# Fused pooled attention and residual MLP on one core: the first batch's loads, scores and order of parts rearranged

## The chip, the core and the metric

The kernel runs on one core of a Trainium2 chip. The metric is the time of one execution in microseconds of device time. Before the change three executions took 329.8, 329.99 and 332.36 us; the median is 329.99 us. A core has five engines that take their instructions in the order written: TensorE (PE, with its weight loads as PEld), VectorE (DVE), ScalarE (ACT), GpSimd (POOL) and SyncE (SP), and 16 DMA engines that move data. DMAs are issued from the queues of SP, ACT ("hardware" queues) or POOL ("software" queue; here the only one that converts fp32 to bf16 on the way).

## What is computed

Eight batches; eight heads of width 64, 576 rows, so 512 columns once the heads are side by side.

```python
def _attn_ref(q, k, v):                    # each (8, 8, 576, 64), fp32
    k_p = k.reshape(B, H, Sp, 8, D).mean(axis=3)      # 72 pooled rows
    v_p = v.reshape(B, H, Sp, 8, D).mean(axis=3)
    scores = scale * np.matmul(q, k_p.transpose(0, 1, 3, 2))
    attn = softmax(scores)                            # over the 72
    return np.matmul(attn, v_p)
def _moe_ref(x, ...):                      # x (8, 576, 512)
    a1 = alpha1 * x + beta1
    tok = np.einsum('ts,bsd->btd', w_tok, a1)         # w_tok 576 x 576
    u = x + lam * tok
    a2 = alpha2 * u + beta2
    ch = np.maximum(a2 @ w_ch1, 0.0) @ w_ch2          # 512 -> 2048 -> 512
    return u + lam * ch
```

## The kernel before

The 8 x 576 rows are cut into 36 chunks of 128, four to a block, nine blocks. While TensorE runs the MLP of block n, the attention of batch n + 1 and its token mix are put between its matmuls: `attention(b)` and the loop over blocks (L1187 on) give each part a due time, and the parts are issued in that order. Nothing overlaps with the attention of batch 0, so it is an opening of its own: the `plan` (L1082 to L1111) names its parts as generators, and the string `order` (L1113 to L1119) is the order in which they are advanced. A name that occurs twice is advanced twice: its matmuls at the first, the copy out of PSUM at the second. Each engine keeps its share of that order.

A head's rows 0 to 511 are laid out four to a partition ("c"), the last 64 rows are kept apart as remainder ("rem"), two to a partition and all heads together. The parts of the opening, by name:

- Loads ahead of the order (L414 to L457): lam and alpha1 on ACT's queue into one partition of `vecs`; the remainder rows of q and k, as fp32, on SP's and ACT's; q and k of heads 0 to 3 (`load_q_bf`, `load_k16`), v, then k and q of heads 4 to 7, v of these, w_tok, all with conversion on POOL's. Behind the constants: w1 (`load_w1(0)`, the first half of w_ch1) and batch 1's q (L1070 to L1072). k of batch 1 is k0, k1 in the order.
- d, dr, K: pooling k on TensorE. k's four rows per partition are paired c, c+1 (d copies row 0 behind row 3 to complete the ring), so that K (`att_K`) needs four matmuls a head. It writes `kpT`, in which the half of a head's query columns that belongs to the other row parity is zero.
- F, Fr: transposes of q (`att_F`, `att_Frem`).
- Sha, Shb (`scores`): the scores of one head, half by half: a matmul over 128 rows and 256 columns, with the remainder's 64 in the second half, then one exponential on ACT for each.
- V: pooling v. A: attention times v, a reciprocal and a product on DVE, into `x_tm`.
- s (`spread_lamal`): lam * alpha1, multiplied on one partition (L478), spread to 128 partitions by an fp32 matmul with a row of ones.
- X, R: x times lam*alpha1 into `xs`, main rows and remainder. b0, b1: the row lam * beta1.
- W, r: w_tok transposed, its row sums. M (`mix_T`): the token mix, plus x, times alpha2. T: its transposes. H, G: the first layer of the MLP for 256 and the other 256 tokens.
- la, ll, lr, lv, l1 to l4, k0, k1: loads of the vectors, remainder, v and k of batch 1, w_ch1 and w_ch2. wa: matmuls on zeros before there is data (`keep_warm`).

A tile of PSUM for a part in `in_pair` comes from two banks of their own, for the others from a pool of six.

## Time and profile before

| | us |
|---|---|
| median of three executions | 329.99 |
| profiled execution, time | 331.57 |
| profiled execution, span (first to last instruction) | 330.1 |
| around the span | 1.47 |
| first transpose of q begins (heads 0 to 3) | 8.24 |
| second load of q lands | 14.92 |
| first token-mix matmul of batch 0 begins | 22.38 |
| its result is read by VectorE | 23.67 |
| first matmul of the MLP begins | 28.16 |

Times are from the start of the span, durations in us unless marked ns. A row of the chain of waits has a start, a length and what lay on the chain; a row of the table by stretches has the stretch, its length, the busy time (and instructions) of TensorE, weight loads, VectorE, ScalarE and GpSimd, the granted TensorE clock, the share of the DMA engines and the GB/s that landed. The share can be above 1 when transfers stand in line. A row of the groups has the line, engine, operation, tiles and forms, count, then busy us and mean ns of one, then the idle time before them and what ended it. Engine busy time of TensorE is modelled and says little of its speed.

### The profile page before, as it was taken

Reading aid. Unit: us, or ns where it says so; the run is one execution under the profiler, and the core shown is the slowest. Engines: PE = TensorE matmul, PEld = TensorE weight load, DVE = VectorE, ACT = ScalarE, POOL = GpSimd, SP = SyncE. Lnnn points to the kernel's source line nnn. Section 1 sums busy time; section 2 is a strip of 40 time slices with the busy share of each in tenths; the row PEclk is TensorE's granted clock in tenths of the full one; section 3 lists DMA queues with packets and bytes.
Section 4 is the critical chain, followed back from the end, with each engine's and each line's share of the span. In section 5 each row is a group of like instructions: output and inputs, shape, how many; then the busy total and the mean of one; then the engine's idle time right before and its main releaser. Section 6 shows DMA issues by size and latency. Waiting matters only on the chain.

```text
span 330.1 us, 6467 instructions
## 1 busy us (share of the span) xinstructions
PE 323.3 (98%) x2469; PEld 206.7 (63%) x2469; DVE 235.9 (71%) x497; ACT 175.6 (53%) x324; POOL 115.5 (35%) x140
## 2 busy tenths in 40 slices
PE   7999999999999999999999999999999999999995
PEld 2677754455544576656775677558755866586584
DVE  5686276997779979786968797787788793263263
ACT  1785999358422961388128802782268225803710
POOL 8667535996247010900280027102510560000000
PEclk9999999999999999999999999999999999999999
DMA  7999989957996893499449943996560025003013
GB/s 107 194 220 290 284 172 222 203 147 174 170 261 108 201 180 105 82 266 181 144 95 230 196 150 80 176 214 148 135 178 0 2 53 159 0 2 127 0 34 95
DMA packets 73514, 47.72 MB, mean 145 GB/s; under 512 B 41181, under 2 KB 63845, under 8 KB 73482
## 3 DMA queue, kind: packets, MB, share of 16 engines
q1 hardware_dynamic: 58876, 34.50, 44.8%
q0 software_dynamic: 14000, 12.40, 22.5%
q10 hardware_dynamic: 606, 0.40, 0.5%
q8 instruction: 19, 0.31, 0.4%
q14 instruction: 13, 0.11, 0.1%
HBM read 38.57 MB, written 9.44 MB: 145 GB/s over the span
## 4 chain that ended last, share of the span: by engine, by line
PE 81%; DVE 7%; DMA 5%; POOL 3%; issue 1%; ACT 1%; SPq 0%; POOLq 0%; DVEq 0%
PE ps_h L931 34%; PE ps_w L1048 23%; PE ps_tok L880 10%; PE ps_ch L952 7%; DMA kT<-k_bf 2%; DMA q_bf<-in_q_dram 2%; PE ps_av L792 2%; PE ps_s L748 2%; DVE w L983 1%; DVE u_sb L885 1%; DVE x_tm L801 1%; DVE H L1017 1%; POOL k_bf L388 1%; DVE u_sb L1066 1%; POOL k_raw L386 1%
## 5 line engine op out<-in xcount | busy, mean ns | idle before, releaser
L931 PE MATMUL ps_h<-u_fm,w 128*128 128x512 bf16 (+2 forms) x608 | 132.7, 368 | 0.5 <-DVE u_sb L962 0.2
L939 ACT ACTIVATE H<-ps_h,bias_cols 128x512 bf16<-128x512 f32 x144 | 98.2, 688 | 55.2 <-PE ps_h L931 53.8
L931 PEld LDWEIGHTS <-w 128*128 128x128 bf16 x608 | 66.1, 114 | 50.7 <-issue 2.2
L1048 PEld LDWEIGHTS <-H 128*128 128x128 bf16 x560 | 53.5, 98 | 10.8 <-DVE u_sb L1066 1.2
L890 ACT CAST u_bf<-u_sb 128x512 bf16<-128x512 f32 x32 | 19.8, 618 | 70.7 <-issue 41.7
L1048 PE MATMUL ps_w<-w,H 128*128 128x256 bf16 x448 | 53.6, 273 | 0.0
L815 POOL TENSOR_TENSOR xs<-x_tm,lamal_bc 128x512 bf16<-128x512 f32 x11 | 13.9, 1270 | 104.8 <-DVE x_tm L801 104.7
L1066 DVE TENSOR_TENSOR u_sb<-u_sb,ps_w 128x512 f32<-128x512 f32 x54 | 36.4, 685 | 17.5 <-PE ps_w L1048 17.0
L880 PE MATMUL ps_tok<-xs,wtT 128*128 128x512 bf16 (+3 forms) x200 | 44.5, 380 | 0.0
L885 DVE TENSOR_TENSOR u_sb<-x_tm,ps_tok 128x512 f32<-128x512 f32 (+1 forms) x40 | 27.3, 684 | 8.9 <-PE ps_tok L880 8.9
L801 DVE TENSOR_TENSOR x_tm<-ps_av,recs 128x320 f32<-128x320 f32 x64 | 31.5, 492 | 2.8
L777 ACT ACTIVATE ET<-ps_s 72x512 f16<-72x512 f32 x56 | 32.3, 592 | 0.0
L952 PE MATMUL ps_ch<-w,H 128*128 128x512 bf16 x128 | 30.4, 379 | 0.0
L880 PEld LDWEIGHTS <-wtT 128*128 128x128 bf16 (+3 forms) x200 | 17.5, 100 | 16.4 <-issue 1.1
L717 DVE TENSOR_TENSOR v_u<-v_u 72x1024 f32<-72x1024 f32 (+1 forms) x24 | 23.6, 985 | 0.2
L799 DVE RECIPROCAL recs<-ps_av 128x5 f32<-128x5 f32 x64 | 12.1, 189 | 16.0 <-PE ps_av L796 15.8
L1048 PE MATMUL ps_w<-w_t,h_s 128*128 128x256 bf16 x168 | 22.6, 273 | 0.0
L952 PEld LDWEIGHTS <-H 128*128 128x128 bf16 x128 | 11.9, 97 | 13.7 <-issue 0.4
L386 POOL TENSOR_TENSOR k_raw<-k_raw 128x512 f32<-128x512 f32 x14 | 18.7, 1334 | 3.2 <-DMA k_raw<-in_k_dram 3.1
L388 POOL TENSOR_TENSOR k_bf<-k_raw 128x512 bf16<-128x512 f32 x14 | 19.1, 1364 | 1.1
L1017 DVE TENSOR_TENSOR h_s<-H 128x1024 bf16<-128x1024 bf16 x21 | 14.6, 697 | 6.3 <-ACT H L939 5.8
L1048 PEld LDWEIGHTS <-h_s 128*128 128x128 bf16 x168 | 16.4, 98 | 4.1
(165 smaller groups left out, 358.8 us busy)
## 6 DMA issues: line engine op xcount, KB each, us to landing
out_dram<-u_sb SPq DMA_DIRECT2D x29, 256.0 KB, 4.2
k_raw<-in_k_dram SPq DMA_DIRECT2D x12, 512.0 KB, 4.3
v_u<-in_v_dram SPq DMA_DIRECT2D x12, 512.0 KB
q_bf<-in_q_dram POOLq DMA_DIRECT2D x16, 256.0 KB, 5.9
w<-in_moe_w_ch_dram POOLq DMA_DIRECT2D x6, 512.0 KB, 14.4
out_dram<-u_sb SPq DMA_DIRECT2D x11, 128.0 KB, 2.2
w<-in_moe_w_ch_dram POOLq DMA_DIRECT2D x1, 1024.0 KB, 13.6
k_raw<-in_k_dram POOLq DMA_DIRECT2D x2, 512.0 KB, 14.7
```

The source lines that it names most:

```text
L386: eng.tensor_tensor(out=raw[:, :, 0:2], in0=raw[:, :, 0:2], in1=raw[:, :, 2:4], op=ALU.add)
L388: eng.tensor_tensor(out=bf, in0=twice[0], in1=twice[1], op=ALU.add)
L717: nc.vector.tensor_tensor(out=out, in0=t[:, :, 0:width], in1=t[:, :, width:2 * width], op=ALU.add)
L777: nc.scalar.activation(out=o, in_=i, func=AF.Exp, bias=0.0, scale=0.125 if b < 3 else 0.125 * 0.125)
L801: nc.vector.tensor_tensor(out=x[:, 1 - odd:6 - odd, dd:dd + D], in0=av[:, :, 0:64], in1=rec.unsqueeze(2).to_broadcast((P, 5, D)), op=ALU.mult)
L880: nc.tensor.matmul(out=ps_tok[p0:p1], lhsT=wtT[0:kk, at, P * c:P * c + p1 - p0], rhs=xs_pool[i][0:kk, sc, :], start=(sc == 0), stop=(sc == 4))
L885: nc.vector.tensor_tensor(out=s["u"][p0:p1, :], in0=x[p0:p1, 1 + c if c < 4 else 5 - 5 * i, :], in1=ps_tok[p0:p1, 0:DM], op=ALU.add)
L931: nc.tensor.matmul(out=ps_h[:, t0:t1 + one], lhsT=w1_of(cc, j), rhs=rhs, start=(cc == 0), stop=(cc == 3))
L939: nc.scalar.activation(out=H4[n, j // 4][:, j % 4, :], in_=ps_h, func=AF.Relu, bias=bias_cols[:, j:j + 1], scale=1.0)
L952: nc.tensor.matmul(out=ps, lhsT=H_of(n, j)[:, 128 * m:128 * m + 128], rhs=w2[j // 4][:, j % 4, :], start=(j == 0), stop=(j == NJ - 1))
L1048: nc.tensor.matmul(out=ps, lhsT=stat(j), rhs=moving(j), stop=(j == 7), start=(first and (pp == 0 or alone) and j == 0), skip_group_check=True)
L1066: nc.vector.tensor_tensor(out=o, in0=o, in1=banks[key, "both"], op=ALU.add)
```

## The change

All of it is in batch 0's opening, up to the first MLP block; the batches behind are issued as before.

- q of heads 0 to 3 comes as fp32 on ACT's queue into a tile that the MLP uses later (`load_q32`), and is cast by ScalarE in two parts (c0, c1). k of heads 0 to 3 comes as fp32 on SP's queue (`load_k`), and VectorE adds its rows (ks: `sum_k`, so far used for later batches), so that K0 has one matmul a head. Heads 4 to 7 keep the loads with conversion and d1. The remainder's q is cast by ScalarE (dq), its k added by VectorE (dr).
- SP's queue carries the small vectors; lam and alpha1 come as 12 rows (three copies of four pieces of 128). VectorE multiplies them and splits the product into three bf16 parts (vm), and four bf16 matmuls spread it.
- `kpT` is gone: `scores(p)` takes two heads in the two row halves (64 partitions each), with one exponential of 72x512 for each half (P0 to P3); the remainder's columns are Q0, Q1.
- Copies change engine: three of four qT copies, V1 to VectorE, K1 and the remainder's qT to ScalarE; X of heads 4, 5 to GpSimd, the remainder of heads 0 to 3 and the multiplication by alpha2 of chunk 0 to VectorE. Two memsets go to GpSimd.
- On POOL's queue the constants come first, then v, k and q of heads 4 to 7, v, w_tok. Then batch 1's first q (q0), w1 (l0), its second q (q1), k0 and k1, by their places in the order, which is new throughout.

```diff
@@ loads
+    def load_q32():
+        bf = work.tile([P, 4, 4, D], BF, tag="q_bf", bufs=4, name="q_bf")
+        raw = work.tile([P, 4, 4, D], FP, tag="H4", bufs=4, name="q_raw")
+        nc.scalar.dma_start(out=raw.rearrange("p h c d -> p h (c d)"), in_=rows(q, 0, 0))
+        st1[0]["q"][0], st1[0]["q_raw"] = bf, raw
+    def cast_q(r, copy):
+        pair = slice(2 * r, 2 * r + 2)
+        copy(out=st1[0]["q"][0][:, pair], in_=st1[0]["q_raw"][:, pair])
...
-    load_vector(0, moe_lam)
-    nc.scalar.dma_start(out=vecs[0:1, 2], in_=moe_alpha1.unsqueeze(0))
-    load_rem(0)
-    load_q_bf(0, 0)
-    load_k16(0, 0)
-    load_vector(1, moe_beta1, nc.sync)
+    load_q32()
+    load_k(0, 0)
...
+    load_rem(0, parts=((0, 0), (1, 0)))
+    load_rem(0, nc.scalar, parts=((0, 1), (1, 1)))
+    thrice = vecs[0:12, 2, 0:256].rearrange("p (i n) -> p i n", i=2)
+    for i, src in enumerate((moe_lam, moe_alpha1)):
+        nc.sync.dma_start(out=thrice[:, i], in_=src.rearrange("(c n) -> c n", n=P).unsqueeze(
+            0).to_broadcast((3, 4, P)))
+    load_vector(0, moe_lam, nc.sync)
+    load_vector(1, moe_beta1, nc.sync)
...
+    nc.gpsimd.memset(xs_pool[1][0:64, 4, :], 0.0)
+    nc.gpsimd.memset(vr16, 0.0)
...
@@ three parts
+    def which_part():
+        one = identity_bf[0:12, 0:12]
+        four = const.tile([12, 4], FP, tag="four", name="four")
+        nc.vector.tensor_reduce(out=four, in_=one.rearrange("p (k c) -> p c k", c=4), op=ALU.add,
+                                axis=AX.X)
+        nc.vector.tensor_copy(out=pick, in_=four.unsqueeze(2).to_broadcast((12, 4, P)))
+        for i in range(2):
+            nc.vector.tensor_reduce(out=less[:, i:i + 1], in_=one[:, 4 + 4 * i:], op=ALU.add,
+                                    axis=AX.X)
+        nc.vector.tensor_scalar(out=less, in0=less, scalar1=-1.0, scalar2=None, op0=ALU.mult)
+    def scale_vector(eng):
+        x = thrice[:, 0]
+        eng.tensor_tensor(out=x, in0=thrice[:, 0], in1=thrice[:, 1], op=ALU.mult)
+        for i in range(2):
+            eng.tensor_copy(out=part, in_=x)
+            eng.scalar_tensor_tensor(out=x, in0=part, scalar=less[:, i:i + 1], in1=x,
+                                     op0=ALU.mult, op1=ALU.add)
+        eng.tensor_copy(out=part, in_=x)
...
-        nc.tensor.matmul(out=ps, lhsT=ones_row, rhs=vecs[0:1, 2, cols])
+        for c in range(2):
+            nc.tensor.matmul(out=ps[:, 128 * c:128 * c + 128], lhsT=pick[:, 2 * half + c],
+                             rhs=part)
@@ pooled k and scores
-        for a, copy in enumerate(copies):
-            yield
-            rows = slice(64 * a, 64 * a + 64)
-            copy(out=kpT_pool[u][rows, a], in_=kp[rows])
+        yield
+        copy(out=kp_pool[u], in_=kp)
...
+    def scores(p):
+        st, u, i = st1[0], p // 2, 2 * p % 4
+        ps = [gp("ps_sc") for _ in range(2)]
+        for h in (i, i + 1):
+            for a in range(2):
+                rows = slice(64 * a, 64 * a + 64)
+                nc.tensor.matmul(out=ps[a][0:SPG, 256 * (h - i):256 * (h - i) + 256],
+                                 lhsT=kp_pool[u][rows, h, :],
+                                 rhs=st["qT"][u][rows, 2 * h:2 * h + 2, :])
+        for a in range(2):
+            yield
+            nc.scalar.activation(
+                out=ET_pool[u][:, i:i + 2, 256 * a:256 * a + 256],
+                in_=ps[a][0:SPG, :].rearrange("p (h i) -> p h i", i=256),
+                func=AF.Exp, bias=0.0, scale=0.125)
...
@@ order
-    load_w1(0)
-    load_q_bf(1, 0)
-    load_q_bf(1, 1)
-    warmed = keep_warm(16)
-    cast_rem(0, nc.vector)
+    warmed = keep_warm(14)
+    which_part()
...
-    for i, copy in enumerate((scalar, scalar, scalar, vector)):
+    for i, copy in enumerate((vector, vector, vector, scalar)):
...
-    for c, eng in enumerate((nc.gpsimd, nc.vector, nc.vector, nc.vector)):
+    for c, eng in enumerate((nc.vector, nc.vector, nc.vector, nc.vector)):
...
+        "wa ks c0 dq dr Fr K0 c1 vm Fr q0 F0 F1 F0 s0 K0 Q0 P0 Q0 F1 Q0 s0 V0 d1 la P1 V0 P0 "
+        "P0 P1 b0 l0 P1 K1 A0 F2 q1 F3 A1 A0 K1 A2 F2 P2 F3 V1 A2 P2 Q1 A3 A1 P3 k0 P2 Q1 k1 "
+        "Q1 V1 X0 s1 P3 A5 W1 A3 P3 s1 A5 A4 A7 W1 A6 W3 A4 lr W2 A7 ve W0 W4 A6 W3 X6 X2 R4 "
+        "r1 W2 r1 r3 r2 W4 X4 R6 R0 W0 M1 r0 M1 ve r3 r2 M1 r0 M0 l1 M3 l2 T1 M0 M0 M3 M3 M2 "
+        "T0 M2 ll T1 T3 T0 H2 M2 H1 H2 T2 H1 T3 T2 H3 H0 H3 lv l3 l4 G3 G1 G2 H0 G3 G0 G1 G2 "
+        "G0 b1")
```

More of the change, by code (lines that the diff above doesn't have):

```diff
@@ L457 @@
     load_wtok()
[L459 removed]
+    vp1_pool, kp_pool, ET_pool = [], [], []
     for i in range(4):
@@ L668, in pool_k, with att_K @@
             in_=rest_sums[:, :, 2 * u:2 * u + 2])
-    def att_K(b, u, *copies):
+    def att_K(b, u, copy):
         st = st1[b]
@@ L1088 @@
             "l3": once(lambda: load_w2(0)), "l4": once(lambda: load_w2(1))}
     for u in range(2):
-        plan[f"d{u}"] = once(lambda u=u: double_k(u))
+        plan[f"q{u}"] = once(lambda u=u: load_q_bf(1, u))
         plan[f"k{u}"] = once(lambda u=u: load_k(1, u, queue=nc.gpsimd))
-    for u, copies in enumerate(((scalar, scalar), (vector, vector))):
-        plan[f"K{u}"] = att_K(0, u, *copies)
+        plan[f"Q{u}"] = scores_rest(u)
+    for u, copy in enumerate((scalar, scalar)):
+        plan[f"c{u}"] = once(lambda u=u, copy=copy: cast_q(u, copy))
@@ L1094 @@
+    for u, copy in enumerate((scalar, scalar)):
+        plan[f"K{u}"] = att_K(0, u, copy)
+    for u, copy in enumerate((vector, vector)):
+        plan[f"V{u}"] = first_V(0, u, copy)
     for u, copy in enumerate((vector, scalar)):
-        plan[f"V{u}"] = first_V(0, u, copy)
-    for u, copy in enumerate((scalar, scalar)):
         plan[f"s{u}"] = spread_lamal(u, copy)
-    for i, copy in enumerate((scalar, scalar, scalar, vector)):
-        plan[f"F{i}"] = att_F(0, i, copy)
+    for i, copy in enumerate((vector, vector, vector, scalar)):
+        plan[f"F{i}"], plan[f"P{i}"] = att_F(0, i, copy), scores(i)
@@ L1108 @@
-    for c, eng in enumerate((nc.gpsimd, nc.vector, nc.vector, nc.vector)):
+    for c, copy in enumerate((scalar, scalar, scalar, scalar, scalar)):
+        plan[f"W{c}"] = setup_wtok(c, copy)
+    for c, eng in enumerate((nc.vector, nc.vector, nc.vector, nc.vector)):
         plan[f"r{c}"] = setup_rowsum(c)
```

135 lines of the change are left out of this document (62 added, 73 removed), and 6 rows, old and new, of the table order.

## The prediction, made before the changed kernel was run

> **What bounds the kernel now.** I read the page first, then the chain of waits in order of time, then a table by stretches of the first microseconds, then the groups of the opening (0 to 28.3 us).
>
> ```profile
> span 330.1 us, 6467 instructions
> PE 323.3 (98%) x2469; PEld 206.7 (63%) x2469; DVE 235.9 (71%) x497; ACT 175.6 (53%) x324; POOL 115.5 (35%) x140
> ```
>
> TensorE is busy almost throughout; no other engine is near that. So a gain has to come from a stretch in which TensorE waits, and the chain (start, length, what) shows one only at the start:
>
> ```profile
> 7.27 7.65 DMA q_bf<-in_q_dram
> ...
> 14.97 0.62 PE ps_q L606 x8
> ...
> 19.58 1.89 ACT wtT L535 x3
> ...
> 21.51 0.44 PE ps_rs L544 x5
> ...
> 22.55 3.25 PE ps_tok L880 x15
> ...
> 27.52 0.59 ACT u_fm L909
> ...
> 28.16 1.04 PE ps_h L931 x8
> ```
>
> The second q load (heads 4 to 7) is issued at 7.27 and lands at 14.92. From there it is 7.4 us to the first token-mix matmul (its weight load is at 22.35) and 13.2 us to the first hidden matmul, at 28.16. Behind 28.16 the chain is TensorE on nearly every row up to 58.5, so a shift of 28.16 is carried on. The load is late because the transfers are full:
>
> ```profile
> 0.00:5.00 5.00, 3.38 (x8) 1.19 (x9) 3.66 (x20) 1.17 (x1) 3.54 (x9) 1.00 0.35 48
> 5.00:8.20 3.20, 2.84 (x9) 0.95 (x7) 1.22 (x4) 0.31 (x2) 3.13 (x8) 1.00 1.34 199
> 8.20:15.00 6.80, 6.19 (x75) 4.16 (x76) 3.92 (x14) 4.83 (x13) 4.49 (x7) 1.00 1.37 191
> 56.00:57.00 1.00, 1.00 (x6) 0.49 (x5) 1.00 (x2) 1.00 (x3) 0.00 (x0) 1.00 1.08 367
> ```
>
> The last two columns are the DMA share and GB/s. Until 5 us only 48 GB/s move; from then on the share is above 1 and 190 to 200 GB/s arrive, mostly bf16 made from twice as many fp32 bytes. Plain fp32 arrives at up to 367 (56 to 57 us). So a 512 KB fp32 block costs 256/195 = 1.3 us cast, and 512/345 = 1.5 us plain.
>
> **Loads.** Removed from POOL: two casting loads (0.97 and 0.76 us of issue). Added: the same blocks as fp32 on ACT's and SP's queues, whose first issues stood at 1.02 and 1.03 and moved bytes from 2 to 3 us. If the engines are full from 2.7 instead of 5 us, 2.3 us of transfer time are used; before, the 240 KB moved by then were worth 240/195 = 1.2. That is 1.1 us gained, less 0.3 for the dearer fp32 and plus up to 0.8 because POOL, rid of two issues, reaches the load of k heads 4 to 7 before 6.47. Bounds: 0 to 2.2; I take 1.2, the middle. Second q: 14.92 - 1.2 = 13.7; k of heads 4 to 7: 13.1 - 1.2 = 11.9. The small vector loads and remainder rows move from ACT's queue to SP's behind the 512 KB k; ACT's own two remainder loads now follow q. With the 6.4 us that one took before, they land at 8.3 to 9.3.
>
> The Trainium skill ("DMA: Bandwidth & Descriptors", Issuing engines are not separate DMA queues) speaks against this part: loads from all queues run on the same 16 engines, so spreading them saves only issue time. The share above 1 agrees for 5 to 15 us, the 0.35 before 5 us is where I differ from it; by that rule alone the term is 0, a rival below.
>
> **VectorE up to the second q.** Its constants ended at 10.17. Gone are the wait for remainder q (2.1) and its cast (0.39), memsets of 1.7 (two each of 0.30, 0.28 and 0.27, the last to POOL) and the one-row product (0.62); new are five small operations of which_part, 1.0 at 0.2 each. They end at 6.4, and the first k lands between 5.3 (1.03 + 4.3, the steady k load) and 7.6 (1.03 + 6.6, the first q now): 6.5. Then in order: sum of k 2 x 0.685 (L1066's size), remainder k 0.36, scale_vector six small operations (154 ns for 32x8, 276 for 64x128) 1.2, two qT copies 2 x 0.425, lamal 0.42, double 0.2, V 0.42, bias row 0.68, head 0's reciprocal and product 0.685: 6.2, so 12.7. The doubling of k waits for its load at 11.9, and V, bias and head 0 stand behind it: 11.9 + 0.2 + 1.8 = 13.9. Either way the second q is the last thing, by a little.
>
> **From the second q to the token mix.** These rows give the sizes:
>
> ```profile
> L801 DVE TENSOR_TENSOR x_tm<-ps_av,recs 128x320 f32<-128x320 f32 x8 | 3.9, 492 | 0.3
> L799 DVE RECIPROCAL recs<-ps_av 128x5 f32<-128x5 f32 x8 | 1.5, 193 | 0.0
> L815 DVE TENSOR_TENSOR xs<-x_tm,lamal_bc 128x512 bf16<-128x512 f32 x2 | 1.3, 684 | 0.0
> L733 ACT ACTIVATE ET<-ps_sc 72x320 f16<-72x320 f32 x8 | 3.1, 432 | 0.2 <-PE ps_sc L730 0.2
> L733 ACT ACTIVATE ET<-ps_sc 72x256 f16<-72x256 f32 x8 | 2.7, 378 | 0.7 <-PE ps_sc L727 0.6
> ```
>
> VectorE: qT copy 0.425, seven heads x 0.685 = 4.8, V 0.42, X of heads 6 and 7 0.68: 6.3, after 0.45 for the transposes. The mix can start at 13.7 + 6.8 = 20.5; its fifth matmul needs the remainders (2 x 0.28 and 0.36 = 0.9), so its result stands at 21.4 + 0.45 = 21.9, against 23.67 before: 1.75 earlier.
>
> ScalarE: sixteen exponentials (5.8 us) become eight of 72x512 (592 ns in later batches) and four of 72x128 (0.22): 5.6, the same. It gains two casts of q (0.62 each), loses one kpT copy and takes K1's from VectorE. After the second q: F3 0.59, P2 and P3 2.4, Q1 0.44, lamal 0.37, W1, W3, W2 1.9, row sum 0.25 = 5.9, under VectorE's 6.8. TensorE: the scores fall from 16 x 0.11 + 8 x 0.08 = 2.4 to about 1.2 (row halves in pairs at 0.056, the later batches' spacing), three-part lamal saves 0.9 of the fp32 matmuls' 1.12, K0 0.6; behind the second q remain F2, F3 0.45, seven heads at 0.15, P2, P3 0.45, V 0.77, w_tok 1.45, three row sums 0.85, small ones 0.5: 5.5, again under 6.8. These savings are hidden, and cost nothing if smaller. POOL: the issue of the first k of batch 1 waits for a landing (before: at 15.51), the second (16.84) likewise; three X of 1.29 follow, one more than before, less 0.73 for the remainder: 15.6 + 0.8 + 3.9 = 20.3, just under 20.5.
>
> **From the mix to the end.** u and u_bf of two chunks are 2.74 on VectorE, but T0 stands behind the fourth mix on TensorE: result + 4.0 + 0.6 copy = 4.65 to the first hidden matmul, against 28.16 - 23.67 = 4.5. The multiplication taken from POOL (1.27) thus buys nothing. Net: 1.75 - 0.15 = 1.6.
>
> The first w1 now queues behind one q block of batch 1 (1.5): it landed at 25.2 and lands at about 25.5, needed at 26.6. The v of batch 1 landed at 40.5, used by TensorE only some 0.7 later, so later stages carry a shift of the loads (1.2) + 0.7 = 1.9 at most. 1.6 fits, with little to spare.
>
> Profiled execution: 331.57 us, of which 330.1 span and 1.47 around it; minus 1.6 gives 329.97. The median of the runs before is 329.99, 1.58 below the profiled one, so I take the same 1.6 from it: 328.4.
>
> **Rivals.**
> 1. Nothing is gained, 330.0. The same bytes cross the same engines (the skill's rule); v and w1 of the next stage are just in time, as above. For: share above 1 from 5 to 47 us. Against: 48 GB/s before 5 us.
> 2. The second q is not the limit. If it lands by 12.3 and the doubling of k by 10.7, VectorE runs through without a gap: 12.7 + 6.3 for the mix, 0.9 and 0.45 to its result at 20.35, 3.3 earlier; less the 0.15, 326.8. With the constants done by 5.5 and k landing at its lower bound, 1.0 less: 325.8. For: the second q would have to gain no more than the sum's upper bound (2.2) and a little. Against: the v of batch 1, which caps the shift at 1.9 unless it gains as much as the second q.
> 3. Slower: the two fp32 loads hold up the software queue. If fp32 arrives not at 345 but at the 195 GB/s of the stretch it is in, each costs 2.6 instead of 1.3, and the second q lands at 13.7 + 2.3 = 16.0; the result of the mix is at 24.2, 0.5 later, and with the 0.15 the time is 330.7. At the 107 GB/s of the page's first slice the 1.3 MB of q, k and remainder rows last until 14.7; remainder k, which VectorE takes in order, then stands in front of everything: 14.7 + 0.36, 3.8 of small work, 0.685, 6.3, 0.9, 0.45 = 27.2, 3.5 late: 333.6. It decides from a landing of the remainder rows after 11. The skill's same page (Queues, rings and completion order) has the engines take turns between queues, which would favour this; no row here shows the turn.
> 4. The score pairs don't run side by side: 1.2 us more on TensorE, hidden under VectorE's 6.8; 328.4 stays.
>
> **Numbers.** Forecast (with 4) 0.46: 327.2 to 329.5. Rival 1: 0.21. Rival 2: 0.17, nearly all of it past 1% (under 326.7). Rival 3: 0.16, most of it at the slow end (over 333.3), since a slow start of the loads holds all that follows. A measurement of this kernel can tell about 1% (3.3 us) from no change. Faster 0.16, same 0.70, slower 0.14. Range 326.0 (near rival 2's end) to 332.0 (between rival 3's ends); about 2 in 10 lie outside.
>
> **What would show it.** Right: more than 48 GB/s before 5 us; second q at 13 to 14.5; VectorE without gaps from there to the mix; result of the mix at 21.9, first hidden matmul at 26.6. Wrong: VectorE waiting for remainder k or for the doubled k beyond 12; ScalarE's transposed w_tok later than VectorE's X; hidden matmuls waiting on w1, or v of batch 1 later than TensorE wants it.

## The result

The changed kernel takes 332.31 us (median of 17 executions, 331.33 to 337.55) against 330.07 for the kernel before, measured in the same series (17 executions, 329.47 to 332.36). The ratio is 1.0076, 95% interval 1.0052 to 1.0100: 0.76% slower, where 1.6 us less was forecast; the median lies 0.3 above the upper end of the range. In all that follows ratios leave out executions over 1.5% above the fastest of the same kernel and medians hold all of them, so the two can differ a little.

The profiled execution of the changed kernel is one of its longer ones, 335.39 us; none near its own median was recorded, which matters below. Its page:

```profile
span 333.9 us, 6397 instructions
PE 319.8 (96%) x2420; PEld 205.3 (61%) x2451; DVE 241.9 (72%) x503; ACT 174.5 (52%) x320; POOL 114.0 (34%) x139
```

TensorE has a little less to do than before in a longer span: 2451 weight loads (x of PEld) against 2469. (31 of its matmuls are missing from this trace, so its busy time is not compared.) Waiting was added. The table by stretches answers to the one shown before; its last row is new:

```profile
0.00:5.00 5.00, 3.49 (x9) 1.29 (x10) 3.08 (x20) 1.49 (x2) 4.05 (x13) 1.00 0.51 164
5.00:8.20 3.20, 2.55 (x15) 1.02 (x13) 2.79 (x10) 1.27 (x3) 3.20 (x6) 1.00 1.30 257
8.20:15.00 6.80, 5.11 (x83) 3.71 (x79) 5.65 (x21) 4.44 (x12) 4.23 (x7) 1.00 1.30 186
19.00:23.00 4.00, 3.98 (x36) 3.13 (x35) 1.91 (x5) 2.58 (x8) 3.63 (x5) 0.57 1.13 212
```

The loads did what was said of them: 164 GB/s land before 5 us instead of 48, and 257 instead of 199 in the next stretch. But from 19.5 to 22.9 us TensorE's granted clock was about half (0.57 in this row's mean), which no trace of the kernel before shows. The chain of waits no longer has a load of q in it:

```profile
7.95 10.73 DMA wt_bf<-in_moe_w_tok_dram
...
22.66 0.41 PE ps_tok L925
...
28.70 2.83 DVE u_bf L937
...
31.98 1.10 PE ps_h L976 x10
```

The opening now ends with w_tok: the second of its three parts is issued at 7.95 and lands at 18.68, 3.8 us before the first token mix at 22.45. VectorE's product of u with alpha2 (`u_bf`), which took 0.69 us for the chunk before, takes 2.8 for the last one, and TensorE waits for it.

### The profile page after: what moved, and what is told of

Read it like the earlier page. It is cut to its first block, busy times and chain, and to the rows that moved or that the text cites. A ratio compares the mean times of both kernels' runs of the same rounds, so it can differ in the third digit from the quotient of the medians.

```text
span 333.9 us, 6397 instructions
## 1 busy us (share of the span) xinstructions
PE 319.8 (96%) x2420; PEld 205.3 (61%) x2451; DVE 241.9 (72%) x503; ACT 174.5 (52%) x320; POOL 114.0 (34%) x139
## 3 DMA queue, kind: packets, MB, share of 16 engines
q0 software_dynamic: 12944, 11.87, 21.5%
## 4 chain that ended last, share of the span: by engine, by line
PE 87%; DVE 5%; DMA 3%; POOL 2%; issue 1%; POOLq 0%
PE ps_h L976 37%; PE ps_w L1093 26%; PE ps_tok L925 10%; PE ps_ch L997 6%; DMA wt_bf<-in_moe_w_tok_dram 3%; PE ps_s L793 2%; PE ps_av L837 2%; DVE w L1028 2%; DVE u_bf L937 1%; DVE u_sb L930 1%; PE ps_r L800 1%; PE ps_w L568 1%; PE ps_rs L581 1%; POOL v L321 1%; PE ps_av L841 1%
## 5 line engine op out<-in xcount | busy, mean ns | idle before, releaser
L976 PE MATMUL ps_h<-u_fm,w 128*128 128x512 bf16 (+2 forms) x588 | 131.0, 368 | 2.5 <-DVE u_sb L1007 1.6
L860 POOL TENSOR_TENSOR xs<-x_tm,lamal_bc 128x512 bf16<-128x512 f32 x12 | 15.2, 1266 | 108.9 <-DVE x_tm L846 108.3
L925 PE MATMUL ps_tok<-xs,wtT 128*128 128x512 bf16 (+2 forms) x193 | 44.6, 381 | 0.4
L997 PEld LDWEIGHTS <-H 128*128 128x128 bf16 x128 | 11.9, 97 | 13.7 <-issue 0.4
L1062 DVE TENSOR_TENSOR H<-H,H 128x1024 bf16<-128x1024 bf16 x14 | 9.6, 689 | 13.3 <-ACT H L984 13.1
```

Source lines behind the costliest of these rows:

```text
L925: nc.tensor.matmul(out=ps_tok[p0:p1], lhsT=wtT[0:kk, at, P * c:P * c + p1 - p0], rhs=xs_pool[i][0:kk, sc, :], start=(sc == 0), stop=(sc == 4))
L976: nc.tensor.matmul(out=ps_h[:, t0:t1 + one], lhsT=w1_of(cc, j), rhs=rhs, start=(cc == 0), stop=(cc == 3))
L997: nc.tensor.matmul(out=ps, lhsT=H_of(n, j)[:, 128 * m:128 * m + 128], rhs=w2[j // 4][:, j % 4, :], start=(j == 0), stop=(j == NJ - 1))
L1062: nc.vector.tensor_tensor(out=o, in0=a, in1=b, op=op)
```

## The experiments

Four theories were put to the test at first: A, that w_tok's landing is the limit; B, that VectorE's products of u with alpha2 run into GpSimd's work for batch 1; C, that the clock dip is the loss; and that nothing but spread between executions was seen. Later came D, a collision in block 1, and E, the spread in three parts in front of the first scores.

**The same kernel again, and three one-part changes.** `e1_again` is unaltered. `e2_gate` makes GpSimd's work for batch 1 wait until the last product with alpha2: its output tile is first written by VectorE at that place in the order. `e3_w0first` changes the transposes of w_tok so that the part that lands last (W3, r3 in place of W0, r0) is used last. `e4_fill` puts matmuls on zeros before the transposes of w_tok, to hold the clock.

```diff
+    def gate_rem():
+        st1[1]["rem"] = (work.tile([P, 2, 2, D], BF, tag="rem_q", bufs=2, name="rem_q"),
...
+        nc.vector.memset(st1[1]["rem"][0][:, 0, 0, 0:1], 0.0)
+    plan["gz"] = once(gate_rem)
...
-        "T0 M2 ll T1 T3 T0 H2 M2 H1 ...
+        "T0 M2 ll T1 T3 T0 H2 M2 gz H1 ...
```

```diff
-        ... W1 A6 W3 A4 lr W2 A7 ve W0 W4 A6 W3 X6 X2 R4 r1 W2 r1 r3 r2 ... R0 W0 M1 r0 M1
+        ... W1 A6 W0 A4 lr W2 A7 ve W3 W4 A6 W0 X6 X2 R4 r1 W2 r1 r0 r2 ... R0 W3 M1 r3 M1
```

> The changed kernel unaltered, for a second profile. Theory A (w_tok is late): TensorE waits for the w_tok load at about 18.7 again, and the first token mix starts no earlier than 21.5, in any execution. Theory B (collision): VectorE's multiplication by alpha2 of the fourth chunk to be mixed is stretched from 0.69 to 2 us or more beside GpSimd's work for batch 1, and the transposes that wait for it come at about 31.5. Theory C (clock): the granted clock is near 0.5 from 19 to 23 us; if this execution has a clock of 1.0 there and its time is still 2 us above before's, C is not the cause. Time 332.3.

> GpSimd's first operation for batch 1 waits for VectorE's last multiplication by alpha2 of the opening; nothing else differs. Theory B: that multiplication is back at 0.7, the hidden layer's second half starts 2 us earlier, time 330.3. Theories A and C: no change, 332.3, since GpSimd's work is not on the chain.

> Chunks 0 and 3 of w_tok change places in the order of transposes and row sums, so that the one that needs the last w_tok load comes last, as before the change. Theory A: TensorE and ScalarE fill the wait at 18 us, the token mix starts about 1 us earlier, time 331.2; with the collision gone because the mix is earlier than GpSimd, 329.3. Theory B alone: as long as the fourth mix is still multiplied after 28.6, 332.3. Theory C alone: the clock stays up if the idle stretch goes, 330.8.

> Four matmuls on zeros (0.9 us) stand where TensorE waits for w_tok; nothing else differs. Theory C: the granted clock stays at 1.0 from 19 to 23 us, 1.5 us are won, time 330.8. Theory A and B: no gain, 332.3 or up to 0.5 more.

Measured beside 330.02: again 334.04, ratio 1.0075 [1.0043, 1.0107]; gate 332.45, 1.0085 [1.0053, 1.0117]; late part last 332.82, 1.0095 [1.0057, 1.0133]; fill 333.35, 1.0082 [1.0049, 1.0114]. The loss repeats (1.0075 after 1.0076); none of the three parts alone takes it away. In the traces of the gate and of the late part last the long product is gone (0.69), and the first matmul of the MLP begins at 27.04 and 26.49 instead of 28.59; their profiled executions are 331.49 and 331.88 us. So theory B's collision is real in the executions that showed it (2.82 us in the changed kernel's, 2.83 in e1's, 2.46 in the fill's, all of them among the longest of their kernels), and yet the typical one is not explained by it. The fill did not keep the clock up: four of its seven executions had a mean granted clock under 0.998, where the changed kernel has nine of 17, and in the recorded one the clock is half from 18.0 to 21.5.

**The kernel before, a second time.** The size of "late" rested on one recorded execution of the kernel before, so another was taken.

> The kernel before, unaltered, for a second trace of it: its recorded execution took 331.57 us where its median is 330.07. If that trace holds a chance loss, this one shows a span of 328.3 to 328.9 us and lacks a loss of about a microsecond somewhere; the 1.9 us that VectorE waited for kT at 212 us (transposed by DMA) is the suspect. If the trace was typical, the span is 329.5 to 330.5 and the two agree stage by stage.

It took 330.3 us (span 328.8) against 331.57 of the first, and its opening is a different one. What TensorE's transposes of q waited for, first recorded execution, then second (view of the tile q_bf; us in total, times; matmuls and their weight loads are counted each, 0.7 and 1.5 us of the 2.2):

```profile
  DMA q_bf<-in_q_dram: 2.2, 4
```

```profile
  DMA k<-in_k_dram: 0.2, 1
```

The wait for q, on which the forecast rests, is not there: the second q lands at 13.18 instead of 14.92, and its transposes begin at 13.24 instead of 14.97, without a wait. In the first execution the whole queue was late: the first q, issued at 1.57 in both, landed at 8.19 against 6.83. The traces of e11, e14 and e18 below, which leave the opening of before as it is, are like the second one: the first q lands at 6.6 to 7.0, the second at 12.9 to 13.8, and the first mix begins at 20.6 to 21.3. The chain of this second execution of the kernel before:

```profile
9.28 9.16 DMA wt_bf<-in_moe_w_tok_dram
...
21.05 0.22 PE ps_tok L880
...
25.49 15.04 DMA v_main<-in_v_dram
```

It is w_tok already here: the same part, issued at 9.28, landed at 18.44. The changed kernel issues it 1.3 us earlier and it lands no earlier (18.68), after 10.73 instead of 9.16 us. And from 25.49 to 40.5 the chain is the load of batch 1's v: a late opening is not carried to the end, but waits for the same v.

From here on each trace is compared with this second trace of before, by the start of the same instruction (own reckoning, us): when the first mix and the first matmul of the MLP begin, then how far the kernel lies behind (+) at that matmul, near 50.6, near 74 and at the last activation of the MLP.

| trace | first mix | first MLP | there | 50.6 | 74 | end |
|---|---|---|---|---|---|---|
| before, first | 22.38 | 28.16 | +1.50 | +0.50 | +0.78 | +1.26 |
| before, second | 20.88 | 26.66 | 0 | 0 | 0 | 0 |
| changed | 22.45 | 28.59 | +1.93 | +3.06 | +4.80 | +4.78 |
| e2_gate | 21.13 | 27.04 | +0.38 | -0.48 | +0.91 | +0.89 |
| e3_w0first | 20.59 | 26.49 | -0.17 | -0.24 | +0.82 | +1.28 |
| e6_both | 20.69 | 26.58 | -0.08 | -0.10 | +1.14 | +1.11 |
| e7_both_w2 | 22.24 | 28.35 | +1.69 | +0.70 | +1.60 | +7.65 |
| e9_m0_gpsimd | 21.04 | 26.94 | +0.28 | +0.12 | +1.53 | +1.51 |
| e10_w2_late | 20.53 | 26.43 | -0.23 | +0.02 | 0.00 | +1.47 |
| e11_before_w2_late | 20.64 | 26.41 | -0.25 | -0.84 | -0.86 | +0.55 |
| e12_w_tok_less | 21.40 | 27.30 | +0.65 | -0.35 | +1.34 | +1.32 |
| e13_w2_idle_pool | 21.98 | 27.88 | +1.22 | +0.34 | +0.77 | +6.03 |
| e14_before_w2_idle_pool | 21.34 | 27.11 | +0.45 | -0.31 | -0.33 | +2.62 |
| e15_spread_later | 21.03 | 26.94 | +0.28 | -0.38 | -0.41 | +6.30 |
| e16_q_software | 25.79 | 32.12 | +5.46 | +4.47 | +6.14 | +6.10 |
| e17_mended | 24.18 | 30.23 | +3.57 | +2.57 | +3.91 | +3.87 |
| e18_before_split | 20.64 | 26.41 | -0.25 | -1.10 | -1.12 | -0.93 |

Two things stand in it. Where the opening of the changed kernel runs well (e3, e6, e9), it ends within 0.3 us of where the kernel before ends it: the change buys nothing there. And every one of these loses 1.1 to 1.4 between 50.6 and 74, with a good opening too; the traces of before, first and second, and of its variants (e11, e14, e18) lose 0.3 there or nothing.

**Both parts together, and two doubled costs.** `e6_both` is e2 and e3 together. `e7_both_w2` is e6 with VectorE's six scalings of w_ch2 by lambda given to GpSimd, at the same due times. `e8_wtok_before_v` is the changed kernel with w_tok's load ahead of the second half of v.

```diff
-                             scale_w2(0, i, nc.vector if on_dve else nc.gpsimd)))
-                todo.append((24.7 + 0.8 * i, lambda i=i: scale_w2(1, i, nc.vector)))
+                             scale_w2(0, i)))
+                todo.append((24.7 + 0.8 * i, lambda i=i: scale_w2(1, i)))
```

```diff
-    load_v16(0, (2,))
     load_wtok()
+    load_v16(0, (2,))
```

> The changed kernel with both edits of the first experiments: the remainder chunk of w_tok transposed first, and GpSimd's work for the next batch held until VectorE has done the fourth multiplication by alpha2. Theory A + B (the opening's loss is the wait for w_tok and the collision of VectorE with GpSimd, and both edits remove them): first hidden matmul at 26.3 to 26.8 us, as with the swap alone (26.49), no multiplication of that group over 0.8 us, bias row no longer 2 us. Theory D (what the opening wins is given back in block 1, where VectorE's scaling of the second weight runs beside GpSimd's sums of k, whose start is set by the landing of k_raw at 57.2 us and not by the compute): median 331.8 to 332.8 all the same, lead of 1.7 us at 58 us and at most 0.3 us at 72 us against the first trace of before. Without D the median is 328.0 to 329.0.

> As the run with both edits, and besides the six scalings of the second weight that VectorE does at 55 to 67 us are put on GpSimd, behind its sums of k. Theory D: VectorE has no multiplication of 1.2 to 1.8 us there any more, TensorE doesn't wait for u_sb at 68 us, and the lead at 72 us stays at 1.5 us or more; median 1.2 to 1.6 us under that of the run with both edits. Rival: the scalings had room on VectorE and GpSimd, busy until 87 us with them, holds up the next loads of q that it issues (now at 78 us): no gain, or 0.5 us lost.

> The changed kernel with one edit: the three loads of w_tok are issued ahead of the load of v's second half on the same queue (0.25 MB, some 1.0 to 1.4 us at the 186 to 257 GB/s of that stretch). Theory A: w_tok lands about 1 us earlier, TensorE's wait of 0.86 + 0.74 us at 18.7 us goes or halves, the granted clock stays at 1.0, and the first hidden matmul comes at 27.3 to 28.0 (28.59 in the changed kernel) unless the multiplication still collides. Rival: v's second half is then late by as much, VectorE's copies of the pooled v wait for it (they begin at 13 us) and the mix starts no earlier. Median 331.5 to 332.8 either way, as the give-back of block 1 stays.

Measured beside 330.44: e6 331.55 (331.45 to 331.73), 1.0034 [1.0017, 1.0050]; e7 338.81, 1.0248 [1.0212, 1.0284]; e8 338.79, 1.0233 [1.0188, 1.0277].

e6 is the best form of the changed kernel that was found, steady within 0.3 us, and still 1.1 us [0.6 to 1.65] behind before. Its recorded opening runs at full clock and level with before; what is left arises in block 1, where TensorE waits in front of the first layer of the MLP:

```profile
68.55 2.75 PE L976 MATMUL ps_h<-u_fm,w 128*128 128x512 bf16 x12 [1.10 <-DVE u_sb L1007]
```

The row names VectorE, but what ended the wait is the transposed u of the block's fourth chunk: TensorE's sequencer waits for that transpose from 65.25 to 68.38, and it lands at 68.34. The transpose is a DMA on SP's queue. There it stands behind the transpose of the remainder of batch 2's q, which needs a cast by GpSimd (`rem_q`), and that cast stands behind GpSimd's four long sums for k of batch 2. GpSimd (first sum, cast), then SP, second trace of before:

```profile
56.24 1.45 POOL L386 TENSOR_TENSOR k_raw<-k_raw 128x512 f32<-128x512 f32 x1 [2.71 <-DMA k_raw<-in_k_dram]
62.36 0.86 POOL L371 CAST rem_q<-rem_raw 128x256 bf16<-128x256 f32 x1
63.24 1.17 SPq L627 DMA_TRANSPOSE rem_qT<-rem_q  x1
64.50 1.22 SPq L901 DMA_TRANSPOSE u_fm<-u_bf  x1
```

The same in e6, with ScalarE's cast of the fourth u, which was ready at 62.34:

```profile
57.51 1.27 POOL L397 TENSOR_TENSOR k_raw<-k_raw 128x512 f32<-128x512 f32 x1 [4.08 <-DMA k_raw<-in_k_dram]
61.72 0.62 ACT L935 CAST u_bf<-u_sb 128x512 bf16<-128x512 f32 x1 [1.14 <-DVE u_sb L930]
63.77 0.85 POOL L388 CAST rem_q<-rem_raw 128x256 bf16<-128x256 f32 x1
64.65 1.17 SPq L664 DMA_TRANSPOSE rem_qT<-rem_q  x1
65.91 1.22 SPq L946 DMA_TRANSPOSE u_fm<-u_bf  x1
```

The transpose is issued 1.41 us later than in before. 1.26 of it is the load of k, which landed at 57.37 against 56.11. 0.13 is GpSimd's work from its first sum to the end of the cast, 7.11 against 6.98. Before has 0.24 to spare, so TensorE begins 1.17 later. In all 13 traces in which TensorE waits at this place, the changed kernel's and its forms', the first matmul begins 2.5 to 2.7 us after this issue. Why the k landed later, though issued earlier (50.83 against 51.46), is not settled; of the 16 parts in which its landing is signalled, 15 were in by 56.10, and the last came at 57.37.

Theory D looked for the loss on VectorE, whose scalings of w_ch2, 0.69 us by themselves, last longer while GpSimd sums. That is so in both kernels, second trace of before and then e6:

```profile
61.79 1.97 DVE L983 TENSOR_TENSOR w<-w,lam_bc 128x512 bf16<-128x512 bf16 x2
```

```profile
61.60 2.77 DVE L1028 TENSOR_TENSOR w<-w,lam_bc 128x512 bf16<-128x512 bf16 x2
```

But the u that VectorE finishes behind them, the remainder's, is transposed only at 68.94, after TensorE has gone on. What the scalings can cost is GpSimd's time beside them.

e7 rid VectorE of the scalings, and GpSimd's work in front of the transpose took 6.23 us instead of 7.11; but its k landed at 58.72, and 0.9 were lost all the same between 50.6 and 74. Then GpSimd's scalings last until 87.39 and its load of q stands behind them (78.56 in e6). That is a dearer wait on top of the one that stayed. e8 answers a question of the opening: with w_tok ahead, the second half of v is issued at 8.3, lands at 21.3, and TensorE waits 6.0 us for it in one piece (in its longest execution, the recorded one). Both loads are needed at about the same time, so this exchange has nothing to give.

**M0 on GpSimd again, the scalings later, w_tok cut.** `e9_m0_gpsimd` undoes one part of the change. `e10_w2_late` is e6 with four of the scalings moved behind block 1's sums, `e11_before_w2_late` is the kernel before with the same move. `e12_w_tok_less` is e6 with one of w_tok's three loads alone; the other two are left out, and all transposes read the part that is there.

```diff
-    for c, eng in enumerate((nc.vector, nc.vector, nc.vector, nc.vector)):
+    for c, eng in enumerate((nc.gpsimd, nc.vector, nc.vector, nc.vector)):
```

```diff
-                todo.append((24.7 + 0.8 * i, lambda i=i: scale_w2(1, i, nc.vector)))
         if n == FIRST - 1:
+            for i in range(4):
+                todo.append((6.0 + 0.8 * i, lambda i=i: scale_w2(1, i, nc.vector)))
```

```diff
-        for c0, c1 in ((0, 2 * S + 64), (2 * S + 64, 4 * S)):
+        for c0, c1 in ((0, 2 * S + 64),):
             nc.gpsimd.dma_start(out=wt_bf[:, c0:c1], in_=main[:, c0:c1])
-        nc.gpsimd.dma_start(out=wt_bf[0:REM, 4 * S:5 * S], in_=moe_w_tok[512:576, :])
```

> The changed kernel with one of its parts undone: the multiplication by alpha2 of the mix's first chunk is GpSimd's again (1.27 us there against 0.69 on VectorE). Theory B: freeing GpSimd is what let its work for batch 1 start at 28.7 us, beside VectorE's last multiplication (2.82 us instead of 0.69); with GpSimd busy for 1.27 us more that work starts later, no multiplication of the group takes over 1.2 us, and TensorE's last chunk of transposes comes within 1 us of where the mix allows (27.9 to 29.0, by when w_tok landed; 31.58 in the changed kernel). Rival: the collision only moves, and another VectorE operation of the stage takes 2 us or more. Median 331.2 to 332.4 (the block-1 loss stays).

> The changed kernel with both edits of the opening, and with VectorE's four scalings of the second group of w2 moved from 60 to 66 us (beside GpSimd's sums of k) into block 1, at 80 to 92 us, where GpSimd is idle. Theory D: the stage 59 to 67 us no longer loses 1.2 us against the second trace of before; first store of block 0 and block 1's first hidden chunk 1.0 to 1.4 us earlier than in the run with both edits; median 330.0 to 330.6, level with before. Rival: VectorE, busy 40 of 47 us in block 1, is delayed there by the added 2.8 us and TensorE waits: median not under 331.4.

> The kernel before with the same move of the four scalings alone. Theory D says that before doesn't lose there in its usual execution (its multiplications fall between GpSimd's sums; 0.6 us lost in its second trace at 59 to 66 us): 0 to 0.6 us gained, 329.6 to 330.3. If it gains as much as the changed kernel does (over 1 us), the loss of block 1 is not the change's.

> The changed kernel with both edits of the opening, but only the first of w_tok's three loads is made, and every chunk of the transposes reads that part (the mix is computed with the wrong weights). This measures what w_tok's landing holds. Theory A (the landing of w_tok at 18.5 to 19.4 us is the next limit behind q, in both kernels): no wait of TensorE for w_tok, the mix starts 0.5 to 1.0 us before the 20.69 of the run with both edits, first hidden matmul at 25.5 to 26.0. Rival: VectorE's chain to the remainders at 20.1 to 20.9 us is the limit at the same time, and the mix starts at 20.4 or later.

Measured beside 330.46: e9 332.52, 1.0061 [1.0032, 1.0091]; e10 332.61, 1.0062 [1.0029, 1.0094]; e11 330.95, 1.0013 [0.9994, 1.0032]; e12 331.94, 1.0059 [1.0020, 1.0097].

e9's trace, at full clock and 0.2 us from the changed kernel's median, shows +0.28 at the first MLP matmul and +1.53 at 74. It is the nearest thing to a typical execution of the changed kernel that was recorded, and the product moved to VectorE is worth nothing in it, as forecast. e10 takes the loss of block 1 away: with the scalings moved it is level with before at 74 (0.00). Its k lands as late as in e6 (57.18), but GpSimd, with fewer scalings beside it, needs 5.87 us instead of 7.11 up to the end of its cast, and the transposed u is issued at 64.47, in time. It does not win it, since the moved scalings then stand on VectorE in front of the attention's reciprocals and products at 74.5 to 79, and 1.15 us are lost at 82. In the kernel before (e11), which does not wait there, the same move gains nothing at 74, and its trace loses 0.9 at 82 likewise; by the times the move costs nothing that can be told. e12 is inconclusive: the landing was early, but its clock fell for 3.4 us from about 12.7 on, and the mix began at 21.40.

**The scalings on GpSimd in its idle time, the spread moved, q by software.** `e13_w2_idle_pool` is e6 with the four scalings on GpSimd at a due time where it was idle; `e14_before_w2_idle_pool` is before with it. `e15_spread_later` is e13 with the spread (vm, s0) behind the copies of the first q. `e16_q_software` is the changed kernel with the first q loaded with conversion by GpSimd's queue, as before.

```diff
-                todo.append((24.7 + 0.8 * i, lambda i=i: scale_w2(1, i, nc.vector)))
...
+            for i in range(4):
+                todo.append((6.7 + 0.01 * i, lambda i=i: scale_w2(1, i)))
```

```diff
-        "wa ks c0 dq dr Fr K0 c1 vm Fr q0 F0 F1 F0 s0 K0 Q0 P0 Q0 F1 Q0 s0 V0 d1 la P1 V0 P0 "
-        "P0 P1 b0 l0 P1 K1 A0 F2 ...
+        "wa ks c0 dq dr Fr K0 c1 Fr q0 F0 F1 F0 K0 Q0 P0 Q0 F1 vm Q0 V0 d1 la P1 V0 P0 s0 P0 "
+        "P1 b0 l0 P1 s0 K1 A0 F2 ...
```

```diff
-    load_q32()
+    load_q_bf(0, 0)
```

> The changed kernel with both edits of the opening, and VectorE's four scalings of the second group of w2 given to GpSimd behind its issue of the next q loads, at 80 to 86 us, where GpSimd is idle for 8 us. Theory D as sharpened by the two moves before (the scalings cost 1.2 us at 59 to 67 us; put on VectorE at 74 to 79 us they cost 1.15 us again at 82, in front of its normalisations; put on GpSimd at 66 to 87 us they held its q loads up by 9 us): level with the second trace of before at 73 us (within 0.2 us) and still level at 90; span 328.6 to 329.2, median 330.0 to 330.8, about 1 us under the run with both edits. Rival: GpSimd's multiplications at 80 to 86 us slow VectorE's sums of v and xs beside them, and 0.5 us or more is lost at 82 to 90.

> The kernel before with that same move alone. It had 0.86 us of lead at 73 us when the scalings were moved to VectorE's block 1, and lost it at 82; here nothing stands in front of VectorE's normalisations: span 327.9 to 328.4, median 0.5 to 0.9 us under the kernel before. If so, the collision of block 1 costs both kernels, and the changed one more.

> As the run that gives the scalings to the idle GpSimd, and in the opening VectorE makes the three bf16 parts of lambda times alpha1 (six operations, 1.77 us at 8.3 to 10.1) behind the two copies of the first qT instead of in front of them, and TensorE spreads them later. Theory E: these six operations are the changed kernel's own cost; TensorE's wait of 1.0 to 1.5 us at 8.8 to 10.3 goes, and with it the execution-by-execution drop of the granted clock to 0.5 at 11 to 16 us seen in two of the profiles; scores begin 0.7 to 1.0 us earlier (10.51), but the mix starts where w_tok lands, within 0.3 us of 20.7. Median equal to the run without this or up to 0.5 us under it, with all clocks at 0.998 or more. Rival: TensorE then waits longer for q's second half and w_tok, and the clock drops there instead.

> The changed kernel with one part undone: q of heads 0 to 3 is loaded by the software queue as bf16, as before, and ScalarE's two casts of it go; k stays fp32 by the hardware queue. Theory A: the opening is held by the software queue's bytes up to w_tok and by the order behind it, and q as fp32 by a second queue bought no earlier mix: the mix starts within 0.6 us of the changed kernel's, w_tok lands 18.5 to 20 us, median 331.5 to 333.5. Rival (the fp32 load of q is a gain, or a loss, of its own): median 0.8 us or more away from the changed kernel's 332.3 in either direction.

Measured beside 330.28: e13 337.57, 1.0222 [1.0190, 1.0254]; e14 333.13, 1.0078 [1.0050, 1.0106]; e15 338.18, 1.0234 [1.0198, 1.0271]; e16 334.6, 1.0116 [1.0078, 1.0154].

In e13 the rival came true. VectorE, then GpSimd:

```profile
79.81 3.43 DVE L860 TENSOR_TENSOR xs<-x_tm,lamal_bc 128x512 bf16<-128x512 f32 x1
```

```profile
79.27 4.99 POOL L1028 TENSOR_TENSOR w<-w,lam_bc 128x512 bf16<-128x512 bf16 x4
```

A product of 0.69 us lasts 3.43 while GpSimd multiplies, and TensorE waits 3.46 us for what follows. The kernel before pays for the same edit (e14: 2.41 for that product), so this is the cost of two engines multiplying at once, not of the change.

e15 tests the spread. In e13 TensorE waits 1.1 us for the three parts before its first scores; with the spread moved the first scores begin at 9.41 instead of 10.51, but TensorE then waits 0.8 for the second copy of q. At the first MLP matmul e15 stands at +0.28 and at 50.6 at -0.38, where e6, with the spread in front, has -0.08 and -0.10: no gain that one trace each could show. (e13 itself is no measure for it: its clock was half from 11.5 to 14.9.)

e16 points to a gain of the fp32 load of q within this change: without it the opening is 5.5 us late, in one trace, with TensorE waiting 1.5 for k and 1.1 for the parts and then at half clock from 13.0 to 26.7. By the times the two kernels' intervals overlap, so the gain itself is not shown.

**A version from what was found, and its control.** `e17_mended` is e6 with the spread moved as in e15 and two of the scalings split off, to 6.0 and 13.3 of block 1; `e18_before_split` is the kernel before with that split alone.

```diff
-                todo.append((24.7 + 0.8 * i, lambda i=i: scale_w2(1, i, nc.vector)))
+                if i < 2:
+                    todo.append((24.7 + 0.8 * i, lambda i=i: scale_w2(1, i, nc.vector)))
         if n == FIRST - 1:
+            for i, at in ((2, 6.0), (3, 13.3)):
+                todo.append((at, lambda i=i: scale_w2(1, i, nc.vector)))
```

> The changed kernel with the edits that helped: the remainder of w_tok first, GpSimd's work for batch 1 behind VectorE's last multiplication, the three-part spread behind the copies of qT, and only two of VectorE's scalings of w2 moved, each into a hole of VectorE where GpSimd doesn't multiply for long (74 to 78 us, 85 to 86 us). The theory (VectorE's operations on two SBUF operands are held while GpSimd multiplies; the opening ends with w_tok): no operation of VectorE over 1.3 us at 61 to 67 us, level with the second trace of before at 73 us (-0.5 to +0.3), no loss over 0.4 us at 79 to 90 us; span 328.3 to 329.3, clock at 0.998 or more in most executions, median 329.8 to 330.8: level with the kernel before, 1.5 to 2.5 us under the changed kernel. Rival: the scalings in the holes collide too (over 1.2 us each) and the loss moves to 79 to 90 us; median 331 or more.

> The kernel before with only the move of those two scalings. Level or up to 0.6 us ahead of its second trace at 73 us, and nothing lost at 79 to 90; median 0.3 to 0.8 us under the kernel before. If it is no faster, the collision of block 1 costs the kernel before nothing, and the 1.2 us there are the changed kernel's alone.

Measured beside 329.98: e17 332.92 (330.69 to 335.79), 1.0069 [1.0039, 1.0100]; e18 329.8, 1.0000 [0.9981, 1.0019]. The recorded execution of e17 has one wait of 1.6 us on TensorE, up to 14.82, and from 14.2 to 24.5 half clock, with TensorE busy all the time from the end of that wait on:

```profile
14.82 0.64 PE L755 MATMUL ps_sc<-qT,kp 64*72 64x256 bf16 x4 [1.59 <-DVE qT L650]
```

```profile
15.00:19.00 4.00, 4.00 (x32) 2.04 (x30) 2.09 (x6) 2.19 (x6) 1.70 (x2) 0.50 1.17 186
```

Block 1 costs it 1.3 us by the same path as e6: its k lands at 60.40 and the transposed u is issued at 68.67, 2.6 us before the first matmul. No form of the changed kernel beats the one before.

## Why the prediction was wrong

**The step that failed is the base of the sum**, in "What bounds the kernel now" and in the last line of the working: that the second q's landing at 14.92 sets the opening, and "so I take the same 1.6 from it" for the median. The second trace of before, and the three of its variants with the same opening, show that the late landing belongs to that one execution: 13.18 (12.9 to 13.8) is usual. It made the opening 1.5 us late, of which 0.50 are left at 50.6, and the profiled execution stood 1.58 above the median: the forecast took away from the median a wait that the median did not hold. The prediction's own line, "1.58 below the profiled one", could have raised the question. The changed kernel's opening by itself came out about as forecast where it runs well: first MLP matmul at 26.5 to 26.9 (26.6 forecast). But before has 26.66 there too.

**Loads** was right in size for the second q: 164 GB/s before 5 us, and a landing at 12.14, 1.0 before the usual 13.18 (1.2 forecast). For heads 0 to 3 it gained nothing: the fp32 q is there for ScalarE's first cast at 6.9, no earlier than the cast q landed before (6.83), and with the casts behind it the transposes begin at 8.42 against 7.10. And it left out w_tok, last in the same queue. Issued 1.3 us earlier, it lands at 18.68 against 18.44. No experiment shows why; in the traces 241 KB arrive over the hardware queues between 15.0 and 18.5 us beside it, against 7 in before, by the load of alpha2 for all partitions, which SP now issues at 11.17 instead of 14.93. The first profile had shown that w_tok counts: the chain's 19.58 is the copy of the transposed w_tok. The page that spoke against this part, the Trainium skill's "DMA: Bandwidth & Descriptors", Issuing engines are not separate DMA queues, agrees with what ends the opening (18.68 against 18.44); in the first 5 us more was moved all the same, 164 GB/s against 48.

**VectorE up to the second q**: the spread in three parts takes 1.77 us (8.31 to 10.08), not 1.2, and TensorE waits 1.0 to 1.5 for it, where the forecast counted VectorE's time only.

**From the second q to the token mix**: VectorE's part was right. The last X begins at 19.60 and ends at 20.29, the remainders run from 20.21 to 21.0, and a mix at 20.6 to 21.0 is what e3, e6 and e9 show. But the kernel before does the same, 20.88, when its q is not late. In the changed kernel's profiled execution the mix is at 22.45: 0.24 from w_tok's landing, the rest from its transposes and row sums at half clock (18.72 to 22.66 is 3.9 us; 18.48 to 21.05 is 2.6 in before).

**From the mix to the end**: "the multiplication taken from POOL buys nothing" was right (e9). That "a shift is carried on" was wrong in both directions. An early or late opening is partly evened out at batch 1's v (+1.50 becomes +0.50 in the first trace of before). A late one can also grow: in the changed kernel's profiled execution GpSimd's sums for batch 1 begin at 28.65, when its q has landed, and a mix that is 1.6 late has its last product of u with alpha2 beside them. VectorE, changed kernel:

```profile
28.70 2.82 DVE L937 TENSOR_TENSOR u_bf<-u_sb,al_bc 128x512 bf16<-128x512 f32 x1
```

GpSimd, same execution:

```profile
29.02 0.73 POOL L391 TENSOR_TENSOR rem_k<-rem_raw 128x256 bf16<-128x256 f32 x1
29.70 1.26 POOL L397 TENSOR_TENSOR k_raw<-k_raw 128x512 f32<-128x512 f32 x1
```

VectorE in e6, where the product comes 2 us earlier:

```profile
26.70 0.69 DVE L937 TENSOR_TENSOR u_bf<-u_sb,al_bc 128x512 bf16<-128x512 f32 x1
```

So 1.93 late at the first MLP matmul becomes 4.1 behind it; about 1.0 is made up at the v (+3.06 at 50.6), and block 1 adds 1.7, by the path shown for e6 (the transposed u issued at 69.56, the first matmul at 72.21).

**The whole, as far as it is accounted for.** e6 lies 1.1 us behind before, and its trace puts 1.2 of that into block 1: the late k of batch 2, GpSimd's sums and SP's order, which the forecast did not look at. The changed kernel lies another 0.76 behind e6 (332.31 - 331.55). Of its 17 executions eight had a granted clock of 0.998 or more over the span, and their median is 332.1; the other nine have 334.1 and reach up to 337.55. So half clock goes with the long executions, and 2.0 of the 2.2 us are there without it. (The kernel before had a mean clock under 0.998 in three of 82 executions.) In the one trace of that kind (e9) the opening's end accounts for 0.28 of 1.5 and block 1 for the rest; that e6 is 0.6 better than such executions, while the gate and the late part last each left the median where it was, is not taken apart further.

**The rivals.** Rival 1, nothing gained, was the nearest, for the reason given there (the same bytes over the same engines), plus a loss elsewhere. Rival 2's condition came true, the second q is not the limit, but its gain did not, because w_tok is. Rival 3 was the right sign by the wrong mechanism: the remainder rows did not come late (VectorE pools remainder k at 7.88, not after 11). Of the signs listed as "wrong", the transposed w_tok later than VectorE's X is the one that appeared.

## What to carry to other kernels

Before a wait is taken as the limit, record the kernel twice: a profiled execution that stands above the median may hold the very wait that is to be removed, and then it must not be taken from the median. Of loads that share the transfer engines, look at the last one that the stage needs, since moving earlier ones only reorders what is in front of it. An engine's new place in time is a cost too: ask what multiplies on GpSimd while VectorE multiplies. And where a row says what ended a wait, follow the data as well: here the row named VectorE, while the data stood in an in-order DMA queue behind work for the next batch.

## What the runs showed of the hardware that was not expected

**VectorE held beside GpSimd.** Products of two SBUF tiles on VectorE, 0.69 us by themselves, took 2.82 (changed), 2.41 (e14) and 3.43 us (e13) when GpSimd multiplied at the same time, and a row of 512 that took 0.74 before took 2.72 in e6; products that read PSUM kept their 0.68. The Trainium skill, "SBUF — State Buffer", Who interferes with whom, states an exclusive lock on a port that the two share, held for one whole instruction. The kind agrees; the size does not quite: in e13 one instruction of GpSimd lasted 1.25 us, and VectorE's product took 2.74 longer than by itself, more than two of them.

**The clock.** TensorE was granted half its clock after idle stretches of 1.6 us at most, for 3.4 us (changed, 19.5 to 22.9), 10.2 (e17) and 13.7 (e16), in the last two while it was busy for all but 0.6 us. e9, with idle stretches of up to 1.34, kept the full clock. The Trainium skill, "TensorE: Matmul & The Clock Gate", What's actually happening, has the clock fall after a whole idle window of some 3.4 us and come back after one busy window. The lengths here are one, three and four times such a window. That an idle window has to come first, and that one busy window ends it, these traces do not bear out; what does decide is open.
